# A routed attention block: the extra unit narrowed to 32 tokens, with tokens stationary in four column strips

## The chip, the core and the metric

The kernel runs on one core of a Trainium2 chip. Its time is the device time of one execution in microseconds (us); a measured time is the median of several runs. The core has TensorE (PE in the profile, with PEld for its weight loads), VectorE (DVE), ScalarE (ACT), GpSimd (POOL) and SyncE (SP, whose queue issues most DMAs).

## What is computed

Three layers, of 8 batches with 576 tokens, 8 heads of 64, so 4608 rows of 512 values. First an attention through 32 packed tokens, then two layers that route every token to one of 8 experts; the second adds its input and skips tokens with a low score:

```
p_packed = sm_attn(p, k, v)
out = sm_attn(q, p_packed, p_packed)
...
x = moe(out)     # e = argmax(x @ w_gate); out = gate * (relu(x @ w1[e]) @ w2[e])
x = moe2(x)      # the same for tokens with x @ w_skip > 0, added to x
```

Hidden size F is 1024. With this case's inputs nearly every token of a batch goes to one expert in the first layer: worked out from the reference, 4607 of the 4608 tokens go to the most frequent expert of their batch, and one, token 326 of batch 1, goes to another.

## The kernel before

All products are fp32 or split into two fp32r parts (names ending in h and l, three matmuls for one product). For each batch `gen_S`, `gen_T` and `gen_R` do the attention and the routing, `gen_pre` forms Q1 = packed values times W1 of the batch's common expert, and `gen_M` the main work: `stage1` (line 649, PE `h`, 48 matmuls for each half of 288 tokens) and `stage2` (line 670, PE `y`, 96 matmuls for each half). The classes `Weave` and `merge` lay side generators between the steps of the main one by a position from 0 to 1. The order that the engines get at the end is what the building program's scheduler makes of it, and it can differ from the order in the code.

Tokens that go to another expert than their batch's common one are handled in extra units. A unit is a group of 64 neighbouring tokens of one batch (`UW` = 64, `NU` = 9 to a batch) with one other expert. `x_flags` (lines 878 to 891) counts for each unit and expert whether a token wants it: five matmuls with `M5` (line 881) and a few DVE operations. `gen_prefix` numbers the flagged units, `x_sel` picks one, `x_load` (lines 916 to 936) issues its loads on SP: packed values (`PK`, stored by line 438 to `pkd`), attention weights of the unit (`A2`), gates (`gB`), then W1 of its expert in four DMAs of 512 KB (line 929) and W2 in four of 512 KB (line 934). Here one unit is flagged. `gen_x` computes it, as a side generator of the first half of the last batch (`first_half`, with `NXS` steps from position 0.25 to 1.0):

- Q1 of the unit's expert: 2 x 8 matmuls on eight tiles of the array (line 366, `q<-eW,xPK`, 512 columns), copied to SBUF by DVE and ACT;
- `h`: 16 matmuls with full 128x128 weights and 64 columns (line 957), relu on DVE and ACT in eight pieces;
- `y`: 16 matmuls, tokens as weights in two strips of 64 columns of the array, 256 columns of W2 each (line 967);
- four transposes (977), `L` (982) for the second layer's routing, `route`, and three accumulating DMAs on POOL (986, 989, 993).

Behind it SP issues the loads of the second layer's first expert into the same buffers (`load0`). The stretch from there on is a chain of such experts, up to the end.

The packed values of each batch go to DRAM in `gen_S`: DVE scales them (`pk`, line 430), PE transposes them (434), ACT copies the result out (`PKT`, 437) and issues the store (438).

Of the kernel before, what the change touches and what calls it, by code (L numbers as in the profile page):

```python
# [24 lines left out]
NU = 9  # L25
UW = 64
# [92 lines left out]
def attn_moe_kernel(ctx, tc, q, k, v, p, wg, w11, w12, w21, w22, out):  # L119
# [31 lines left out]
    M5 = ct("M5", [128, 5, NXB])  # L151
# [4 lines left out]
    valx = ct("valx", [NXB, B, 3])  # L156
    valy = ct("valy", [64, 32])
    GM = [ct(f"GM{i}", [128, 5, 32]) for i in range(2)]
    GMx = ct("GMx", [32, 2, 32])
# [28 lines left out]
    def gen_consts():  # L188
        for t, x in ((sel, 0.0), (valy, 0.0), (GMx, 0.0), (FM, 0.0), (FX, 0.0), (csx, 0.0)):
# [4 lines left out]
        stp, q8, m8, bid, R2 = (  # L194
            ct("c_" + n, shp)
            for n, shp in (("stp", [128, 16]), ("q8", [128, 1]), ("m8", [128, 1]), ("bid", [NXB, B]), ("R2", [128, 4, E]))
# [5 lines left out]
        iota_f(bid, [[1, B]], 0, 0)  # L202
# [10 lines left out]
        nc.vector.tensor_copy(valx[:, :, 1], q8[0:NXB, :].to_broadcast([NXB, B]))  # L213
        yield
        nc.vector.tensor_copy(valx[:, :, 2], m8[0:NXB, :].to_broadcast([NXB, B]))
# [9 lines left out]
        for i, c in enumerate(LC):  # L225
            for s in range(i % 2, 5):
                u = (c // 32 + s) // 2
                nc.gpsimd.tensor_copy(
                    M5[32 * i:32 * i + 32, s, E * u:E * u + E], E8[32 * i:32 * i + 32, :]
                )  # L230
            yield
# [139 lines left out]
    def gen_S(b):  # L371
# [66 lines left out]
        nc.scalar.dma_start(out=pkd[b], in_=PKT)  # L438
# [439 lines left out]
    def x_flags():  # L878
        f0 = mt("f0")
        for s in range(5):  # L880
            nc.tensor.matmul(out=f0[0:NXB, 0:B], lhsT=M5[:, s, :], rhs=csA[:, s, :], start=(s == 0), stop=(s == 4))
        FL = X["FL"]
        nc.vector.tensor_scalar(
            out=FL, in0=kmA[0:NXB, :], scalar1=-1.0, scalar2=float(E), op0=ALU.mult, op1=ALU.add
        )
        nc.vector.tensor_tensor(out=FL, in0=FL, in1=valx[:, :, 2], op=ALU.not_equal)
        nc.vector.scalar_tensor_tensor(
            out=FL, in0=f0[0:NXB, 0:B], scalar=0.0, in1=FL, op0=ALU.is_gt, op1=ALU.mult
        )
        nc.tensor.matmul(out=f0[0:32, 64:64 + B], lhsT=ones[0:NXB, 0:32], rhs=FL, start=True, stop=True)  # L890
        nc.vector.tensor_copy(X["cnt"], f0[0:32, 64:64 + B])

    def x_prep(X, b0, nb):
        X["b0"], X["nb"] = b0, nb
        X["fc"] = X["FL"][:, b0:b0 + nb]
        X["pc"] = yield from gen_prefix(X["fc"], nb, NXB)
        nc.vector.memset(X["ctr"], 0.0)

    def x_sel(X):
# [9 lines left out]
            in1=o[:, 0:nb].unsqueeze(1).to_broadcast([NXB, 3, nb]), op=ALU.mult,  # L909
# [3 lines left out]
        nc.tensor.matmul(out=l0[0:64, 0:3], lhsT=ones[0:NXB, 0:64], rhs=r5, start=True, stop=True)  # L913
# [24 lines left out]
    def gen_x(X):  # L938
        li = X["li"]
        A2g = X["A2"]  # L940
        nc.vector.tensor_tensor(out=A2g, in0=A2g, in1=X["gB"].unsqueeze(1).to_broadcast([128, 2, UW]), op=ALU.mult)
        Q1 = EB["X"].rearrange("p t c -> p (t c)")[:, 0:2 * F].rearrange("p (g f) -> p g f", g=2)
        for n in range(2):
            sl = slice(512 * n, 512 * n + 512)
            ps = [mt("q1") for _ in range(2)]
            heads(ps, X["PK"], lambda hp: EB["W1"][:, hp, sl], start=True, stop=True)
            for g in range(2):
                if g:
                    nc.scalar.copy(out=Q1[:, g, sl], in_=ps[g])
# [42 lines left out]
        gT = yield from route("x", L[0:32, 0:UW], 32, 2, GMx, True)  # L992
# [17 lines left out]
    NXS = 4 + 4 + 2 + 2 + 14 + 4  # L1010
# [236 lines left out]
    for b in range(B):  # L1247
# [19 lines left out]
        if b == B - 2:  # L1267
# [8 lines left out]
            for n, shp in (("PK", [128, 128]), ("A2", [128, 2, UW]), ("gB", [128, UW]), ("h", [128, 8, UW]),  # L1276
# [299 lines left out]
```

## Time and profile before

| what | value |
|---|---|
| median of 3 runs | 621.17 us (620.44 to 621.42) |
| the profiled execution | 618.02 us |
| its span, first to last instruction | 616.4 us |
| PE busy in the span | 588.2 us (95%) |
| DVE, ACT, POOL busy | 339.4, 213.3, 133.1 us |
| DMA, mean over the span | 198 GB/s |
| mean granted PE clock | 0.986 |

The profile is of one execution, and it was 3.15 us under the median. Busy shares are means over stages with different limits; what a change is worth in one stage is read from that stage: which work or wait ends last there.

### The profile page before, as it was taken

How to read it: one execution, taken by the hardware profiler on the slowest of the kernel's cores; microseconds unless marked ns; L12 is line 12 of the kernel's file. 1: busy time of each engine (PE TensorE's matmuls, PEld its weight loads, DVE VectorE, ACT ScalarE, POOL GpSimd, SP SyncE). 2: the span in 40 equal slices, each digit the busy share in tenths (PEclk: the TensorE clock that was granted, in tenths of full speed). 3: DMA queues.
4: the chain of work that ended last, by engine and by line, in shares of the span. 5: the costliest groups of instructions: out<-in, count | busy, mean ns of one | idle time of the engine just before them, and what ended most of it. 6: DMA issues, size and time to landing. Idle time of an engine off the chain costs nothing.

```text
span 616.4 us, 14334 instructions
## 1 busy us (share of the span) xinstructions
PE 588.2 (95%) x5737; PEld 529.2 (86%) x5738; DVE 339.4 (55%) x978; ACT 213.3 (35%) x463; POOL 133.1 (22%) x121
## 2 busy tenths in 40 slices
PE   4698999999999999999999999999999899999996
PEld 2287899899989989989988988799999899999796
DVE  2796738738737746845855854346656166253111
ACT  3352542442362343254244134215424135043110
POOL 3123151060150141132123114020301230140032
PEclk9698999999999999999999999999999999999998
DMA  8918788676477566637435415959137581732065
GB/s 341 346 56 311 282 305 325 224 255 240 175 253 252 211 238 237 252 113 283 177 100 216 178 60 191 342 117 401 33 111 281 76 356 27 236 58 113 1 92 64
DMA packets 35994, 122.18 MB, mean 198 GB/s; under 512 B 5696, under 2 KB 15680, under 8 KB 29888
## 3 DMA queue, kind: packets, MB, share of 16 engines
q1 hardware_dynamic: 30064, 113.56, 50.0%
q0 software_dynamic: 3968, 4.98, 6.4%
q10 hardware_dynamic: 1872, 2.49, 1.2%
q8 instruction: 50, 0.82, 0.5%
q14 instruction: 40, 0.33, 0.2%
HBM read 91.62 MB, written 29.39 MB: 196 GB/s over the span
## 4 chain that ended last, share of the span: by engine, by line
PE 68%; issue 11%; another core or an unknown queue 7%; DVE 5%; DMA 4%; POOL 2%; POOLq 1%; ACT 1%; SPq 0%; DVEq 0%; ACTq 0%
PE y L670 33%; PE h L649 18%; PE y L1225 4%; PE q L366 3%; PE s L366 3%; PE L L706 2%; DMA out_dram<-iXR 2%; POOL iW2l L567 1%; PE pv L422 1%; PE at L411 1%; DMA kT<-in_k_dram 1%; DMA W2c<-in_w_dram 1%; PE L L523 1%; DMA W1c<-in_w_dram 1%
## 5 line engine op out<-in xcount | busy, mean ns | idle before, releaser
L670 PE MATMUL y<-hh,W2h 128*128 128x288 f32 x512 | 156.5, 306 | 1.9 <-ACT W2h L566 1.9
L670 PE MATMUL y<-hh,W2l 128*128 128x288 f32 x512 | 151.5, 296 | 0.7 <-DVE W2l L567 0.7
L670 PE MATMUL y<-hl,W2h 128*128 128x288 f32 x512 | 151.8, 296 | 0.0
L670 PEld LDWEIGHTS y<-hh,W2h 128*128 128x128 f32 x512 | 97.0, 189 | 18.9 <-issue 13.5
L567 POOL TENSOR_TENSOR W2l<-W2c,W2h 128x1024 fp32r<-128x1024 f32 x30 | 72.4, 2413 | 156.5 <-ACT W2h L566 121.8
L670 PEld LDWEIGHTS y<-hh,W2l 128*128 128x128 f32 x512 | 97.0, 190 | 1.0 <-DVE W2l L567 1.0
L670 PEld LDWEIGHTS y<-hl,W2h 128*128 128x128 f32 x512 | 96.8, 189 | 0.1
L655 DVE SCALAR_TENSOR_TENSOR hl<-h,hh 128x288 fp32r<-128x288 f32 x128 | 57.9, 455 | 43.4 <-ACT hh L654 43.0
L654 ACT ACTIVATE hh<-h 128x288 fp32r<-128x288 f32 x128 | 52.6, 412 | 80.4 <-PE h L649 80.2
L649 PE MATMUL h<-A2h,Q1h 128*128 128x288 f32 x256 | 78.3, 306 | 0.0
L649 PE MATMUL h<-A2l,Q1h 128*128 128x288 f32 x256 | 75.5, 295 | 0.0
L649 PE MATMUL h<-A2h,Q1l 128*128 128x288 f32 x256 | 75.3, 294 | 0.0
L649 PE MATMUL h<-eXh,eW1h 128*128 128x288 f32 x192 | 57.8, 301 | 3.9 <-issue 3.3
L1225 PE MATMUL y<-ihh,iW2h 128*128 128x288 f32 x192 | 56.8, 296 | 0.0
L1225 PE MATMUL y<-ihh,iW2l 128*128 128x288 f32 x192 | 56.6, 295 | 0.0
L1225 PE MATMUL y<-ihl,iW2h 128*128 128x288 f32 x192 | 56.5, 294 | 0.0
L649 PE MATMUL h<-eXl,eW1h 128*128 128x288 f32 x192 | 56.5, 294 | 0.0
L649 PE MATMUL h<-eXh,eW1l 128*128 128x288 f32 x192 | 56.5, 294 | 0.0
L687 DVE TENSOR_TENSOR y<-y,gB 128x288 f32<-128x288 f32 x64 | 28.6, 447 | 44.7 <-PE y L670 42.1
L649 PEld LDWEIGHTS h<-A2h,Q1h 128*128 128x128 f32 x256 | 48.0, 187 | 3.8 <-issue 2.3
L566 ACT CAST W2h<-W2c 128x1024 fp32r<-128x1024 f32 x32 | 33.6, 1051 | 49.3 <-DMA W2c<-in_w_dram 19.5
L649 PEld LDWEIGHTS h<-A2h,Q1l 128*128 128x128 f32 x256 | 48.1, 188 | 0.0
(289 smaller groups left out, 948.7 us busy)
## 6 DMA issues: line engine op xcount, KB each, us to landing
W2c<-in_w_dram SPq DMA_DIRECT2D x32, 512.0 KB
eW<-in_w_dram SPq DMA_DIRECT2D x8, 2048.0 KB
W1c<-in_w_dram SPq DMA_DIRECT2D x30, 512.0 KB
kT<-in_k_dram SPq DMA_DIRECT2D x7, 1152.0 KB
qT<-in_q_dram SPq DMA_DIRECT2D x7, 1152.0 KB
v<-in_v_dram SPq DMA_DIRECT2D x7, 1152.0 KB
x2d<-y SPq DMA_DIRECT2D x7, 1152.0 KB
out_dram<-y SPq DMA_DIRECT2D x7, 1152.0 KB
```

The costliest lines, as they stand in the source:

```text
L366: nc.tensor.matmul(out=out[x][32 * hp:32 * hp + 32], lhsT=lhsT[64 * x:64 * x + 64, 32 * hp:32 * hp + 32], rhs=rhs(hp)[64 * x:64 * x + 64], ...
L411: nc.tensor.transpose(ats[x][:, 128 * j:128 * j + 128], a1[:, x, 128 * j:128 * j + 128], ident)
L422: nc.tensor.matmul(out=pv[x][32 * hp:32 * hp + 32], lhsT=aT[:, 4 * x + j, 32 * hp:32 * hp + 32], rhs=vm[:, 2 * hp + x, j, :], start=(j == ...
L566: nc.scalar.copy(out=hi, in_=x)
L567: eng.tensor_tensor(out=lo, in0=x, in1=hi.bitcast(F32), op=ALU.subtract)
L649: nc.tensor.matmul(out=ps[:, 0:nr], lhsT=l[:, t, 128 * f:128 * f + 128], rhs=r[:, t, :], start=(n == 0), stop=(n == 3 * kt - 1),)
L654: nc.scalar.activation(out=hh[:, f, :], in_=ps[:, 0:n_], func=ACTF.Relu)
L655: nc.vector.scalar_tensor_tensor(out=hl[:, f, :], in0=ps[:, 0:n_], scalar=0.0, in1=hh[:, f, :].bitcast(F32), op0=ALU.max, op1=ALU.subtract,)
L670: nc.tensor.matmul(out=ps[:, 0:HALF], lhsT=l[:, f, :], rhs=r[:, f, :], start=(n == 0), stop=(n == 23))
L687: nc.vector.tensor_tensor(out=y1[:, t, cols], in0=ps[:, 0:HALF], in1=d["gB"][:, cols], op=ALU.mult)
L706: nc.tensor.matmul(out=L[32 * i:32 * i + 32, 0:LN], lhsT=wgB[:, t, :], rhs=y1[:, t, LC[i]:LC[i] + LN], start=(t == 0), stop=(t == 3),)
L1225: nc.tensor.matmul(out=ps[:, 0:HALF], lhsT=l[:, f, 128 * t:128 * t + 128], rhs=r[:, f, c], start=(n == 0), stop=(n == 23))
```

## The change

Units become 32 tokens wide (`UW` = 32, `NU` = 18). So that a unit and an expert still fit in 72 partitions, `M5`, the flags and the lists get a second index for the even or odd unit of a pair; `x_flags` has two groups of five matmuls, and the prefix over six batches has twelve columns instead of six.

`gen_x` no longer forms Q1. It writes attention weights times gate into a block-diagonal tile `bd` (cleared once), forms the values of the unit's tokens (`xt`, two matmuls with the packed values as weights), multiplies them with W1, the tokens being the weights in four strips of 32 columns of the array (`h`, 16 matmuls of 256 columns), does the relu in one ACT operation, transposes back (`hT`, two), multiplies with W2 in four strips (`y`, 32 matmuls of 128 columns), copies out and transposes once (`ro`). For `xt` the packed values are needed untransposed, so `pkd` now stores `pk`, and its DMA is issued on ACT ahead of the transpose. `NXS` falls from 30 to 25. Stores of whole batches move the same bytes as before; the loads of the unit's `A2` and `gB` and its additions move half of theirs.

```diff
-NU = 9
-UW = 64
+UW = 32
+NU = S // UW
+NXP = NU // 2 * E
...
+        nc.scalar.dma_start(out=pkd[b], in_=pk.rearrange("p x d -> p (x d)"))
...
-        nc.scalar.dma_start(out=pkd[b], in_=PKT)
...
     def x_flags():
         f0 = mt("f0")
-        for s in range(5):
-            nc.tensor.matmul(out=f0[0:NXB, 0:B], lhsT=M5[:, s, :], rhs=csA[:, s, :], start=(s == 0), stop=(s == 4))
+        for z in range(2):
+            for s in range(5):
+                nc.tensor.matmul(
+                    out=f0[0:NXP, B * z:B * z + B], lhsT=M5[:, s, z, :], rhs=csA[:, s, :], start=(s == 0), stop=(s == 4)
+                )
...
     def gen_x(X):
         li = X["li"]
-        A2g = X["A2"]
-        nc.vector.tensor_tensor(out=A2g, in0=A2g, in1=X["gB"].unsqueeze(1).to_broadcast([128, 2, UW]), op=ALU.mult)
-        Q1 = EB["X"].rearrange("p t c -> p (t c)")[:, 0:2 * F].rearrange("p (g f) -> p g f", g=2)
-        for n in range(2):
-            sl = slice(512 * n, 512 * n + 512)
-            ps = [mt("q1") for _ in range(2)]
-            heads(ps, X["PK"], lambda hp: EB["W1"][:, hp, sl], start=True, stop=True)
-            for g in range(2):
-                if g:
-                    nc.scalar.copy(out=Q1[:, g, sl], in_=ps[g])
-                else:
-                    nc.vector.tensor_copy(Q1[:, g, sl], ps[g])
-                yield
-        hx, yx = X["h"], X["y"]
-        for f in range(8):
-            ps = mt("h")
-            for g in range(2):
-                nc.tensor.matmul(out=ps[:, 0:UW], lhsT=Q1[:, g, 128 * f:128 * f + 128], rhs=A2g[:, g, :],
-                                 start=(g == 0), stop=(g == 1))
-            if f % 2:
-                nc.scalar.activation(out=hx[:, f, :], in_=ps[:, 0:UW], func=ACTF.Relu)
-                yield
-            else:
-                nc.vector.tensor_scalar(out=hx[:, f, :], in0=ps[:, 0:UW], scalar1=0.0, scalar2=None, op0=ALU.max)
+        A2g, bd, xt, hr, hx, ro, yx = (X[n] for n in ("A2", "bd", "xt", "hq", "hx", "rq", "y"))
+        for hp in range(4):
+            r = slice(32 * hp, 32 * hp + 32)
+            nc.vector.tensor_tensor(
+                out=bd[r, :, hp, :], in0=A2g[r], in1=X["gB"][r].unsqueeze(1).to_broadcast([32, 2, UW]), op=ALU.mult
+            )
+        yield
+        ps = mt("xt")
+        for x in range(2):
+            nc.tensor.matmul(
+                out=ps[64 * x:64 * x + 64, 0:4 * UW], lhsT=X["PK"][:, 64 * x:64 * x + 64],
+                rhs=bd[:, x].rearrange("p h c -> p (h c)"), start=True, stop=True,
+            )
+        nc.vector.tensor_copy(xt, ps[:, 0:4 * UW].rearrange("p (h c) -> p h c", h=4))
+        yield
+        ps = mt("h")
+        for hp in range(4):
+            for z in range(4):
+                nc.tensor.matmul(
+                    out=ps[UW * z:UW * z + UW, 0:256], lhsT=xt[:, hp, :], rhs=EB["W1"][:, hp, 256 * z:256 * z + 256],
+                    start=(hp == 0), stop=(hp == 3),
+                )
+        nc.scalar.activation(out=hr, in_=ps[:, 0:256], func=ACTF.Relu)
+        yield
+        ps = mt("hT")
+        for j in range(2):
+            nc.tensor.transpose(ps[:, 128 * j:128 * j + 128], hr[:, 128 * j:128 * j + 128], ident)
+        nc.vector.tensor_copy(hx, ps[:, 0:256])
+        yield
         ps = mt("y")
         for f in range(8):
-            for n in range(2):
+            j, z = f % 2, f // 2
+            for n in range(4):
                 nc.tensor.matmul(
-                    out=ps[64 * n:64 * n + 64, 0:256], lhsT=hx[:, f, :], rhs=EB["W2"][:, f, 256 * n:256 * n + 256],
-                    start=(f == 0), stop=(f == 7),
+                    out=ps[UW * n:UW * n + UW, 0:128], lhsT=hx[:, 128 * j + UW * z:128 * j + UW * z + UW],
+                    rhs=EB["W2"][:, f, 128 * n:128 * n + 128], start=(f == 0), stop=(f == 7),
                 )
-            if f % 4 == 3:
-                yield
-        nc.scalar.copy(out=X["ro"][0:UW, 0:256], in_=ps[0:64, 0:256])
-        nc.vector.tensor_copy(X["ro"][0:UW, 256:512], ps[64:128, 0:256])
+        nc.scalar.copy(out=ro, in_=ps[:, 0:128])
+        yield
         ps = mt("ro")
-        for t in range(4):
-            nc.tensor.transpose(ps[:, UW * t:UW * t + UW], X["ro"][0:UW, 128 * t:128 * t + 128], ident[0:UW, 0:UW])
+        nc.tensor.transpose(ps[:, 0:128], ro, ident)
         nc.vector.tensor_copy(yx, ps[:, 0:4 * UW].rearrange("p (t c) -> p t c", t=4))
         yield
...
-        gT = yield from route("x", L[0:32, 0:UW], 32, 2, GMx, True)
+        gT = yield from route("x", L[0:32, 0:UW], 32, 1, GMx, True)
...
-    NXS = 4 + 4 + 2 + 2 + 14 + 4
+    NXS = 7 + 14 + 4
...
+            X["bd"] = X["ro"][:, 256:512].rearrange("p (x h c) -> p x h c", x=2, c=UW)
+            nc.vector.memset(X["bd"], 0.0)
```

The scheduler puts the new operations on PE as follows. Before, the end of the unit (PE, first half of the last batch; `h` of line 957 stands in three such pieces of 4, 8 and 4 matmuls ahead of this, each with six main matmuls `y` of line 670 behind it; `eW_5225` is the unit's W2):

```order
L670 MATMUL y<-hh,W2h 128x288
L670 MATMUL y<-hl,W2h 128x288
L670 MATMUL y<-hh,W2l 128x288
L967 MATMUL y<-eW_5225,xh 64x256 x16
L670 MATMUL y<-hh,W2h 128x288
L670 MATMUL y<-hl,W2h 128x288
L670 MATMUL y<-hh,W2l 128x288
```

After, its beginning on PE: the last main matmuls of `stage1` (now line 655), the products with the unit's values and with its W1 (`eW_5227`), and the first main matmuls of `stage2` (now line 676):

```order
L655 MATMUL h<-A2h,Q1h 128x288
L655 MATMUL h<-A2l,Q1h 128x288
L655 MATMUL h<-A2h,Q1l 128x288
L964 MATMUL xt<-xro,xPK 64x128 x2
L973 MATMUL h<-eW_5227,xro 32x256 x16
L676 MATMUL y<-hh,W2h 128x288
L676 MATMUL y<-hl,W2h 128x288
L676 MATMUL y<-hh,W2l 128x288
```

`xt` and `h` stand back to back, behind the whole of `stage1`, where the first Q1 product stood six main matmuls earlier. Then, still on PE, with the transposes `hT` and six main matmuls ahead of what is shown, the product with W2 (`eW_5228`):

```order
L676 MATMUL y<-hh,W2h 128x288
L676 MATMUL y<-hl,W2h 128x288
L676 MATMUL y<-hh,W2l 128x288
L988 MATMUL y<-eW_5228,xh 32x128 x32
L676 MATMUL y<-hh,W2h 128x288
L676 MATMUL y<-hl,W2h 128x288
L676 MATMUL y<-hh,W2l 128x288
L995 MATMUL ro<-ident,xro 128x128
```

Twelve main matmuls of `stage2` now stand between `h` and `y`, and none ahead of `h`; before, 24 stood ahead of `y`.

On ACT the store of the packed values moves, here in the third batch, between evictions of `h` in `gen_M` (`hh`). Before:

```order
L412 COPY aT<-at 128x512 x2
L414 COPY aT<-at 128x128
L654 ACTIVATE hh<-h 128x288 x8
L437 COPY PKT<-ps 128x128
L438 DMA pkd<-PKT 128x128
L286 ACTIVATE ex<-d 128x40
```

After:

```order
L418 COPY aT<-at 128x512 x2
L420 COPY aT<-at 128x128
L660 ACTIVATE hh<-h 128x288
L437 DMA pkd<-pk 128x128
L660 ACTIVATE hh<-h 128x288 x7
L444 COPY PKT<-ps 128x128
L292 ACTIVATE ex<-d 128x40
```

The store now stands behind the first eviction, ahead of seven, where it stood behind the PKT copy.

## Rows read from the trace of the kernel before

**Rows 1.** The page: busy time, share, instructions by engine.

```profile
PE 588.2 (95%) x5737; PEld 529.2 (86%) x5738; DVE 339.4 (55%) x978; ACT 213.3 (35%) x463; POOL 133.1 (22%) x121
```

**Rows 2.** Chain that ended last, in order of time: start us, us, what.

```profile
85.50 0.87 PE at L411 x8
...
385.87 1.02 PE q L366 x16
...
387.88 1.97 PE q L366 x16
...
390.85 0.84 PE h L957 x8
...
392.54 1.73 PE h L957 x16
...
396.82 3.60 PE y L967 x32
...
411.88 6.42 PE h L649 x48
...
424.70 1.21 PE L L706 x16
```

**Rows 3.** Timeline of PE's weight loads: start, us, line, shape, count, idle before.

```profile
387.81 0.15 PEld L366 LDWEIGHTS q<-eW,xPK 64*32 64x32 f32 x8 [0.17 <-issue]
388.79 0.15 PEld L366 LDWEIGHTS q<-eW,xPK 64*32 64x32 f32 x8 [0.83 <-DMA eW<-in_w_dram]
```

**Rows 4.** Timeline of SP's queue: the four W2 loads of the unit.

```profile
382.06 8.31 SPq L934 DMA_DIRECT2D eW<-in_w_dram  x4
```

**Rows 5.** Stretches: busy us by engine, PE clock, DMA share, GB/s.

```profile
388.80:395.70 6.90, 6.90 (x62) 6.06 (x58) 1.53 (x6) 1.26 (x4) 0.00 (x0) 1.00 1.02 288
```

**Rows 6.** Line 967, the old y: the waits that PE's queue executes (ns, times).

```profile
L967 PEldq EVENT_SEMAPHORE  x2: 51/51/51, 394.5 to 395.7; - x2
```

**Rows 7.** Timeline of ACT in the batch before last.

```profile
332.44 0.41 ACT L654 ACTIVATE hh<-h 128x288 fp32r<-128x288 f32 x1 [1.66 <-PE h L649]
...
334.34 0.26 ACT L437 COPY PKT<-ps 128x128 f32<-128x128 f32 x1
334.64 0.34 ACTq L438 DMA_DIRECT2D pkd<-PKT  x1
```

**Rows 8.** Timeline of PE: the flags, and the start of the last half.

```profile
355.42 0.76 PE L881 MATMUL f<-csA,M 128*72 128x8 f32 x10
356.03 0.38 PE L649 MATMUL h<-A2h,Q1h 128*128 128x288 f32 x1
...
411.72 0.29 PE L649 MATMUL h<-A2h,Q1h 128*128 128x288 f32 x1
```

**Rows 9.** Timeline of DVE in the first batches.

```profile
31.57 0.18 DVE L503 TENSOR_SCALAR sm<-sm 128x18 f32<-128x18 f32 x1
```

**Rows 10.** PE's waits in the whole span: us in total, times, longest.

```profile
PE s L366 <- ACT PKT L437: 0.4, 1, 0.4
```

**Rows 11.** Stretches, columns as in rows 5: around the fall, and a gap.

```profile
49.70:52.90 3.20, 0.84 (x5) 0.38 (x3) 1.58 (x2) 1.94 (x2) 0.00 (x0) 1.00 1.01 412
52.90:56.40 3.50, 3.20 (x13) 3.20 (x14) 3.50 (x6) 0.83 (x2) 2.93 (x1) 0.51 1.03 434
...
486.40:493.30 6.90, 4.23 (x32) 4.03 (x31) 0.59 (x2) 3.21 (x4) 2.19 (x3) 1.00 0.57 92
```

**Rows 12.** Timeline of PE: ends of the two gaps, pace of main matmuls.

```profile
51.94 0.40 PE L670 MATMUL y<-hh,W2h 128*128 128x288 f32 x1 [1.93 <-ACT W2h L566]
...
53.61 0.44 PE L670 MATMUL y<-hh,W2h 128*128 128x288 f32 x1
53.85 0.44 PE L670 MATMUL y<-hl,W2h 128*128 128x288 f32 x1
...
56.43 0.29 PE L670 MATMUL y<-hh,W2h 128*128 128x288 f32 x1
...
491.12 0.37 PE L649 MATMUL h<-eXh,eW1h 128*128 128x288 f32 x1 [2.67 <-issue]
```

More of the change, by code (lines that the diff above doesn't have):

```diff
@@ L150, in attn_moe_kernel @@
     E8 = ct("E8", [128, E])
-    M5 = ct("M5", [128, 5, NXB])
+    M5 = ct("M5", [128, 5, 2, NXP])
     once = ct("once", [128, 5, 32])
@@ L193, in gen_consts @@
         yield
-        stp, q8, m8, bid, R2 = (
+        stp, q8, m8, bid, par, R2 = (
             ct("c_" + n, shp)
-            for n, shp in (("stp", [128, 16]), ("q8", [128, 1]), ("m8", [128, 1]), ("bid", [NXB, B]), ("R2", [128, 4, E]))
+            for n, shp in (("stp", [128, 16]), ("q8", [128, 1]), ("m8", [128, 1]), ("bid", [NXP, 2 * B]), ("par", [NXP, 2 * B]), ("R2", [128, 4, E]))
         )
@@ L201, in gen_consts @@
         iota_f(stp, [[-8, 16]], -8, 1)
-        iota_f(bid, [[1, B]], 0, 0)
+        iota_f(bid, [[1, B], [0, 2]], 0, 0)
+        iota_f(par, [[0, B], [1, 2]], 0, 0)
         yield
@@ L212, in gen_consts @@
         nc.vector.tensor_copy(valx[:, :, 0], bid)
-        nc.vector.tensor_copy(valx[:, :, 1], q8[0:NXB, :].to_broadcast([NXB, B]))
+        nc.vector.scalar_tensor_tensor(
+            out=valx[:, :, 1], in0=q8[0:NXP, :].to_broadcast([NXP, 2 * B]), scalar=2.0, in1=par,
+            op0=ALU.mult, op1=ALU.add,
+        )
         yield
-        nc.vector.tensor_copy(valx[:, :, 2], m8[0:NXB, :].to_broadcast([NXB, B]))
+        nc.vector.tensor_copy(valx[:, :, 2], m8[0:NXP, :].to_broadcast([NXP, 2 * B]))
         nc.vector.tensor_copy(valy[:, 0:1], q8[0:64, :])
@@ L879, in x_flags @@
         f0 = mt("f0")
-        for s in range(5):
-            nc.tensor.matmul(out=f0[0:NXB, 0:B], lhsT=M5[:, s, :], rhs=csA[:, s, :], start=(s == 0), stop=(s == 4))
+        for z in range(2):
[3 more added lines that the diff above has]
+                )
         FL = X["FL"]
+        Fv = FL.rearrange("p (b z) -> p b z", z=2)
         nc.vector.tensor_scalar(
-            out=FL, in0=kmA[0:NXB, :], scalar1=-1.0, scalar2=float(E), op0=ALU.mult, op1=ALU.add
+            out=Fv, in0=kmA[0:NXP, :].unsqueeze(2).to_broadcast([NXP, B, 2]), scalar1=-1.0, scalar2=float(E),
+            op0=ALU.mult, op1=ALU.add,
         )
@@ L887, in x_flags @@
         nc.vector.scalar_tensor_tensor(
-            out=FL, in0=f0[0:NXB, 0:B], scalar=0.0, in1=FL, op0=ALU.is_gt, op1=ALU.mult
-        )
-        nc.tensor.matmul(out=f0[0:32, 64:64 + B], lhsT=ones[0:NXB, 0:32], rhs=FL, start=True, stop=True)
-        nc.vector.tensor_copy(X["cnt"], f0[0:32, 64:64 + B])
+            out=Fv, in0=f0[0:NXP, 0:2 * B].rearrange("p (z b) -> p b z", z=2), scalar=0.0, in1=Fv,
+            op0=ALU.is_gt, op1=ALU.mult,
+        )
+        nc.tensor.matmul(out=f0[0:32, 64:64 + 2 * B], lhsT=ones[0:NXP, 0:32], rhs=FL, start=True, stop=True)
+        nc.vector.tensor_reduce(
+            out=X["cnt"], in_=f0[0:32, 64:64 + 2 * B].rearrange("p (b z) -> p b z", z=2), op=ALU.add, axis=AX.X
+        )
     def x_prep(X, b0, nb):
+        b0, nb = 2 * b0, 2 * nb
         X["b0"], X["nb"] = b0, nb
         X["fc"] = X["FL"][:, b0:b0 + nb]
-        X["pc"] = yield from gen_prefix(X["fc"], nb, NXB)
+        X["pc"] = yield from gen_prefix(X["fc"], nb, NXP)
         nc.vector.memset(X["ctr"], 0.0)
@@ L912, in x_sel @@
         l0 = mt("l0")
-        nc.tensor.matmul(out=l0[0:64, 0:3], lhsT=ones[0:NXB, 0:64], rhs=r5, start=True, stop=True)
+        nc.tensor.matmul(out=l0[0:64, 0:3], lhsT=ones[0:NXP, 0:64], rhs=r5, start=True, stop=True)
         nc.vector.tensor_copy(X["li"], l0[0:1, 0:3])
@@ L1275, in attn_moe_kernel @@
             EB["X"] = ep.tile([128, 4, S], F32, name="eX")
-            for n, shp in (("PK", [128, 128]), ("A2", [128, 2, UW]), ("gB", [128, UW]), ("h", [128, 8, UW]),
-                           ("y", [128, 4, UW]), ("ro", [128, DM]), ("ctr", [NXB, 1]), ("o", [NXB, B]), ("ov", [NXB, 3, B]),
-                           ("r5", [NXB, 3]), ("FL", [NXB, B]), ("cnt", [32, B]), ("pcu", [NXB, B]), ("ppc", [NXB, B]),
+            for n, shp in (("PK", [128, 128]), ("A2", [128, 2, UW]), ("gB", [128, UW]), ("h", [128, DM]), ("y", [128, 4, UW]), ("ro", [128, DM]), ("ctr", [NXP, 1]),
+                           ("o", [NXP, 2 * B]), ("ov", [NXP, 3, 2 * B]), ("r5", [NXP, 3]), ("FL", [NXP, 2 * B]),
+                           ("cnt", [32, B]), ("pcu", [NXP, 2 * B]), ("ppc", [NXP, 2 * B]),
                            ("cT", [32, 32]), ("fl", [32, UW])):
@@ L1348, in early @@
                 us[b]["L"] = mt("L")
-                store(b, 0, 4)
+                store(b, 0, 8)
                 logits(b, 0, 1)
@@ L1354, in attn_moe_kernel @@
             W.run(0.84)
-            store(b, 4, NU, 0, 2)
+            store(b, 8, NU, 0, 2)
             W.run()
@@ L1358, in attn_moe_kernel @@
             W.run()
-    store(B - 1, 4, NU, 2, 3)
-    store(B - 1, 4, NU, 3, 4)
+    store(B - 1, 8, NU, 2, 3)
+    store(B - 1, 8, NU, 3, 4)
     logits(B - 1, 2, 3)
```

18 lines of the change are left out of this document (12 added, 6 removed).

## Prediction

> **What bounds the kernel now.** I read the page first: TensorE (PE) is busy for 95% of the span [rows 1], so time is won only where PE's own row gets shorter or where PE waits. The chain that ended last says the same of the stretch that the change touches: between 378 and 432 us every piece of it is PE work. The extra unit (one pass of `gen_x`, for the single token of batch 1 whose expert is not the batch's common one) stands there as seven pieces between the main matmuls of the last batch [rows 2]: the two Q1 products, 1.02 and 1.97 us; the four pieces of `h`, which make 3.41 us (0.84, 1.73 and once more 0.84); and `y`, 3.60 us. The six matmuls between the two Q1 products are main work. The main matmuls cost 6.42 us for 48, 0.134 us each. The main work of the first half (48 and 96 matmuls, some 19.3 us) and the 1.2 us of a logits group leave about 12.4 us of the 33 us between 378.7 and 411.7 us to the extra unit.
>
> The second thing to see is that the unit's weights come late. The second Q1 product lasts twice as long as the first because its last eight weight loads wait 0.83 us for the fourth chunk of W1, until 388.79 us [rows 3]. Behind that chunk come four chunks of W2, 512 KB each: their issue alone ends at 390.37 us [rows 4], and the DMA engines are full, at 288 GB/s, until 395.7 us [rows 5]. 2.10 MB at that rate is 7.3 us, so the last chunk lands near 396.1 us; the two waits that PE's queue executes for the old `y` are at 394.5 and 395.7 us [rows 6], and the old `y` began at 396.8 us without a wait. I take 395.7 us for the landing. Today this costs nothing, since enough work lies ahead of `y`.
>
> **Part 1, the unit itself.** I follow PE from 385.8 us, where the unit's first product begins now [rows 2]. The order of the changed kernel puts six main matmuls there (0.8 us, to 386.6), then `xt` and `h` back to back. `xt` is two matmuls of 128 columns, about 0.3 us. Between them PE has nothing to do while DVE copies 128x128 values out; the nearest row for that is the PKT copy on ACT, 0.26 us [rows 7], with hand-overs 0.45 us: `h` starts near 387.35. For `h` and `y` I need the price of four column strips side by side. The logits row is that shape (128x32 weights, four strips): 16 matmuls of 160 columns in 1.21 us [rows 2], so 640 columns of four strips, 1.9 ns a column. The old `y`, with two strips, gives 2048 columns in 3.60 us, 1.76 ns; the Q1 product 512 columns in 1.02 us, 2.0 ns. The new `h` (4 x 256) and the new `y` (8 x 128) are 1024 columns each: 1.8 to 2.05 us, I take 1.9, the logits row being the same shape. The first half of `h` ends near 388.3, the second needs the W1 chunk of 388.79, and `h` ends at 389.7. Six main matmuls (390.6) cover the relu on ACT (128x256; the 128x288 one takes 0.41 us, rows 7). Two transposes `hT` (eight take 0.87 us, rows 2) with their switch bring 390.9; six more matmuls, under which DVE copies `hT`, bring 391.75. There PE meets `y`, whose first four matmuls need all four W2 chunks. **PE stands from 391.75 to 395.75 us, 4.0 us of a new wait.** `y` ends at 397.65. Left are 84 main matmuls (12 of the 96 of this half ran before `y`, where 24 did) for 11.2 us, one transpose, `L` and their hand-overs, 0.7 us: the half ends at 409.55 where it ended at 411.72 us, the start of the next half [rows 8]. Gain 2.2 us; without the wait it would be 6.2.
>
> **Part 2, what is added elsewhere.** The flags take ten matmuls instead of five. Five cost PE 355.42 to 356.03 us, 0.61 us, in a stretch where PE is full [rows 8]: 0.6 us more, and everything behind moves with it, the loads of the unit too, since they are issued behind work that PE paces. The twelve prefix additions where there were six lie on DVE, between main evictions, and the order places the last of them ahead of the last eviction before `p0`: nothing. The first batches get two small DVE operations ahead of the reciprocal that POOL waits for, of the kind of [rows 9]: 0 to 0.2 us, I take 0.15. The store to `pkd` now stands ahead of evictions on ACT, and waits there for DVE's `pk`; it takes 0.34 us of the queue, and ACT is idle 1.66 us at that place [rows 7]. PE's list of waits has twelve entries; none is for an eviction of `h`, and the one for the PKT copy is 0.4 us, once [rows 10]: nothing. The larger M5 fill, the cleared `bd` and the smaller units of the DMAs lie beside other work: nothing. The loads for the first expert of the second layer, behind the unit's additions on SP, are issued earlier than before; PE does not wait for them now, so nothing is won by that.
>
> **Part 3, the clock.** [...] A gap of 2.67 us at 488.5 us, between full matmuls, brought no fall [rows 11, 12]. [...] At the lower level a main matmul starts every 0.24 us instead of 0.13 [rows 12]; 3.4 us of it hold 14 matmuls and not 25.5, a loss of 1.5 us; if a part of the low stretch falls into the wait, 0.9 us; if all of `y` lies in it, 1.7. I take 1.4.
>
> [...]
>
> **The sum** is made on the profiled execution (618.02 us, span 616.4), 3.15 us under the median of 621.17 us (620.44 to 621.42); I carry the differences over to the median. -2.2 (unit) +0.6 (flags) +0.15 (first batches) +1.4 (clock) = -0.05: **621.1 us**, no change.
>
> **Rivals.**
> R1, the clock stays up. For it: the gap of 2.67 us that brought no fall, and the moment of a fall may depend on more than the gap. Against it: the fall behind 1.93 us. Then 621.1 - 1.4 = 619.7 us.
> R2, the clock stays low for a second stretch, because `y` and what follows at half speed is again not dense. Another 1.5 us: 622.6 us, slower by 0.23%. It decides from the point where the low level lasts more than 5 us. Against it: the one fall inside the span was over within 3.5 us although PE was not full there [rows 11].
> R3, W2 lands before PE gets there, the wait is absent and the clock stays up: 621.1 - 1.4 - 4.0 = 615.7 us. Against it: the DMA engines have no idle share to give [rows 5].
> R4, the strips do not run side by side, and the change does not do what it says: `h` and `y` then cost four times as much, 5.7 us more each, of which the wait swallows 4.0: 11.4 - 4.0 - 1.4 = 6.0 us more, 627 us. The logits row speaks against it.
>
> **How the numbers follow.** Forecast 0.52, R1 0.25, R2 0.13, R3 0.06, R4 0.04. 0.2% is 1.24 us, about what a measurement of this kernel can tell from no change: below 619.93 is faster, above 622.41 slower. The forecast's own spread (columns at 1.8 or 2.05 ns: 0.25 us for each product, only `y` counting; clock 0.9 to 1.7; first batches 0 to 0.2; the landing 395.7 to 396.7) is 620.2 to 622.3; of its 0.52 I give 0.04 to faster, 0.44 to same, 0.04 to slower. R1 lies on the line: 0.15 faster, 0.10 same. R2: 0.03 same, 0.10 slower. R3 is faster, R4 slower. Faster 0.25, same 0.57, slower 0.18. The range reaches from R1 with half a microsecond below it, 619.2, to R2, 622.7.
>
> **What would show it.** In the new trace: `h` near 1.9 us with a pause at its middle; a gap of about 4 us on PE ahead of the unit's `y`, put down to the DMA of W2; `y` near 1.9 us at full clock or 3.5 at the lower; a granted clock of about 0.5 for some 3.4 us somewhere between 394 and 402 us; the flags at about 1.2 us; the first half ending 1.4 us earlier than before without the fall, and about where it ended with it. I am wrong if the gap is under 2 us (then W2 is faster than its row), or if the clock stays at 1.00 through it.

## The result and the profile after

| kernel | median, us | span of the profiled execution, us |
|---|---|---|
| before | 621.19 (620.44 to 621.42) | 616.4 |
| changed | 613.94 (612.21 to 614.12) | 612.5 |

The ratio is 0.9869, with a 95% interval of 0.985 to 0.9888: 7.25 us faster, where no change (621.1) was forecast and 619.2 was the lower end of the range.

Up to the end of the first layer the trace holds nearly what was forecast. These are the new unit's instructions on PE's timeline of the changed kernel (start us, us, what, count, idle before); they answer to the pieces in [rows 2]:

```profile
387.34 0.44 PE L964 MATMUL xt<-xro,xPK 128*64 128x128 f32 x4
389.64 1.93 PE L973 MATMUL h<-eW,xro 128*32 128x256 f32 x32 [1.86 <-issue]
392.42 0.38 PE L981 MATMUL hT<-ident,xh 128*128 128x128 f32 x2
393.53 0.41 PE L988 MATMUL y<-eW,xh 128*32 128x128 f32 x4
395.13 0.41 PE L988 MATMUL y<-eW,xh 128*32 128x128 f32 x2 [1.19 <-DMA eW<-in_w_dram]
396.69 2.61 PE L988 MATMUL y<-eW,xh 128*32 128x128 f32 x58 [1.15 <-DMA eW<-in_w_dram]
400.11 0.41 PE L995 MATMUL ro<-ident,xro 128*128 128x128 f32 x1
401.34 0.44 PE L1000 MATMUL L<-xy,wgAB 128*32 128x32 f32 x8
```

PE stands for 4.20 us in three parts, and the clock falls behind them. In the stretches of the changed kernel (columns as in [rows 5]) PE was busy for 1.56 of 3.9 us; then come 3.4 us at the lower level, a granted clock of 0.50, with PE full:

```profile
393.90:397.80 3.90, 1.56 (x44) 1.25 (x46) 0.00 (x0) 0.00 (x0) 0.00 (x0) 1.00 0.95 336
397.80:401.20 3.40, 3.40 (x34) 2.90 (x26) 0.29 (x1) 0.27 (x1) 0.03 (x1) 0.50 0.99 412
401.20:404.60 3.40, 3.40 (x31) 3.22 (x30) 2.37 (x15) 0.21 (x1) 2.61 (x3) 1.00 0.68 122
```

The time was won behind the unit. The chain of the changed kernel (start us, us, what) begins the last half at 412.24 (before: 411.88, [rows 2]) and its last logits at 432.84, where before they began at 432.49: 0.35 us later than before. The row of before:

```profile
432.49 1.24 PE L L706 x16
```

The changed kernel then runs into the second layer on PE alone:

```profile
412.24 6.41 PE h L655 x48
...
432.84 1.23 PE L L712 x16
434.08 0.63 issue
434.71 12.88 PE h L655 x96
...
462.51 22.26 PE y L1243 x168
```

In what follows the second layer is counted from its first matmul to PE's last: 434.33 to 610.49 us before, 176.2 us, and 434.71 to 606.47 us in the changed kernel, 171.8 us. At the end of its first item stood the gap of 2.67 us of [rows 11, 12], which the trace puts down to "issue". It is gone. This is the stretch of the changed kernel with the same bounds as in [rows 11], PE busy for 6.90 us of 6.90 instead of 4.23:

```profile
486.40:493.30 6.90, 6.90 (x54) 6.90 (x53) 3.63 (x6) 5.02 (x7) 2.17 (x3) 1.00 0.59 103
```

That gap lies at a branch. The line of code that decides which item comes next, L1499 before and L1522 in the changed kernel, has a COMPARE_BRANCH on each engine (count, shortest/median/longest ns, first and last start). First before, where PE's sequencer (PEldq) spends 3.58 us in it:

```profile
L1499 PEldq COMPARE_BRANCH  x1: 3583/3583/3583, 487.0 to 487.0; - x1
```

then the changed kernel:

```profile
L1522 PEldq COMPARE_BRANCH  x1: 453/453/453, 486.4 to 486.4; - x1
```

The trace also shows transfers of instructions. The page of the changed kernel has two queues of that kind; all 11,501 matmuls and weight loads of PE, with its waits and branches, against 49 transfers of 16 KB on q8 make some 235 or more to a transfer, so I take q8 for the queue that brings PE's instructions:

```profile
PE 582.9 (95%) x5750; PEld 527.4 (86%) x5751; DVE 332.7 (54%) x984; ACT 211.0 (34%) x458; POOL 133.7 (22%) x122
...
q8 instruction: 49, 0.80, 0.5%
q14 instruction: 40, 0.33, 0.2%
```

Before, none ran on q8 from 482.5 to 488.0 us, and one from 488.0 to 489.4, in the middle of the branch (DMA view of that stretch: packets, MB, share):

```profile
q8 instruction: 1, 0.02, 4.4%
```

In the changed kernel one had come at 482.5 to 484.0, ahead of the branch:

```profile
q8 instruction: 1, 0.02, 3.9%
```

### The profile page after: what moved, and what is told of

Same layout as the page of the kernel before. It is cut to its first block, busy times and chain, and to the rows that moved or that the text cites. A ratio compares the mean times of both kernels' runs of the same rounds, so it can differ in the third digit from the quotient of the medians.

```text
span 612.5 us, 14364 instructions
## 1 busy us (share of the span) xinstructions
PE 582.9 (95%) x5750; PEld 527.4 (86%) x5751; DVE 332.7 (54%) x984; ACT 211.0 (34%) x458; POOL 133.7 (22%) x122
## 4 chain that ended last, share of the span: by engine, by line
PE 66%; issue 10%; another core or an unknown queue 7%; DMA 7%; DVE 3%; SPq 3%; POOL 2%; ACT 1%; POOLq 0%; ACTq 0%
PE y L676 31%; PE h L655 19%; PE y L1243 4%; PE q L372 3%; PE s L372 3%; DMA out_dram<-iXR 2%; PE L L712 2%; PE pv L428 1%; PE at L417 1%; SPq L949 1%; DMA eW<-in_w_dram 1%; DMA kT<-in_k_dram 1%; PE L L529 1%; DMA out_dram<-ero 1%
## 5 line engine op out<-in xcount | busy, mean ns | idle before, releaser
L655 PEld LDWEIGHTS h<-A2l,Q1h 128*128 128x128 f32 x256 | 48.1, 188 | 0.4 <-DVE A2l L573 0.4
```

The costliest lines, as they stand in the source:

```text
L655: nc.tensor.matmul(out=ps[:, 0:nr], lhsT=l[:, t, 128 * f:128 * f + 128], rhs=r[:, t, :], start=(n == 0), stop=(n == 3 * kt - 1),)
```

## The theories

**F, code fetch.** The change moves PE's code. Counted over the program with a matmul as two instructions, the second layer's first item starts at instruction 7557 before and at 7572 in the changed kernel (that count is too low where matmuls are fp32, as the experiments show). By this theory PE's branch behind it, 3.58 us against 0.45, waits in the one place for a transfer of its target's code and not in the other; nothing that the unit computes matters. The expectations count in pieces of 256 instructions. The traces have transfers of 16 KB on q8, and in before some 254 of PE's instructions to one (7357 to 29, worked out below), 64.6 bytes each.

**U, the unit.** Its additions end earlier, so the second layer's first loads start 2.4 us earlier (407.18 instead of 409.60 us on SP), and that takes waits away behind it.

Instructions in branches that are not taken tell them apart: they move the code behind them and add nothing to execute.

## Experiments

**Eight matmuls in a branch not taken, old unit (e1).**

```diff
             x_loop(X, 0, cnt2)
+            pad = mt("pad")
+            for _ in range(8):
+                nc.tensor.matmul(out=pad[0:32, 0:8], lhsT=ones[:, 0:32], rhs=ones[:, 0:8], start=True, stop=True)
```

> The kernel before, with eight 32x8 matmuls added in a branch that is not taken (inside the one for further extra units, ahead of the second layer's code): nothing more is executed, but the code of TensorE behind it lies 17 instructions further on, about where the change puts it (15). Theory F (code fetch): the gain of 7 us comes from where TensorE's code lies against its 16 KB instruction transfers, so this alone brings it: no 2.67 us pause of PE at 488 us, span 613 to 613.5 instead of 616.4, timed median 613.5 to 614.5. Theory U (the unit: its lighter work ends earlier, and the second layer's loads, 2.4 us earlier, take waits away behind it): nothing moves, span 616.4, median 621.2 within 0.6. VectorE's code is not moved, so its 3.3 us pause at 436.4 should stay under either.

615.22 us (ratio 0.9904, 0.9875 to 0.9934), span 613.5. The branch takes what it takes in the changed kernel, with the old unit, so F holds for most of the gain:

```profile
L1502 PEldq COMPARE_BRANCH  x1: 453/453/453, 487.6 to 487.6; - x1
```

and the second layer, from its first matmul to PE's last, takes 172.9 us instead of 176.2. The changed kernel needs 171.8; 1.1 us are missing. DVE's pause stayed, as expected, and PE now waits for it (waits of this kernel on PE from 430 us on: us in total, times, longest):

```profile
PE f L798 <- DVE f L751: 0.8, 1, 0.8
```

**The other way round: 120 such matmuls, new unit (e2).**

> The changed kernel, with 120 such matmuls in the branch not taken: TensorE's code behind it lies 242 instructions further on, which in pieces of 256 (16 KB at 64 bytes) is 14 back, so within one instruction of where it lay before the change. Theory F: the 2.67 us pause at 488 comes back, span 615.5 to 617, median 620 to 622, so about the time before the change. Theory U: the unit and its loads are as in the changed kernel, so span 612.5 and median 613.9 within 0.6.

616.72 us (0.9932, 0.9906 to 0.9957), span 615.1. The long branch is back, but at 1.86 us and not 3.6, and the kernel is 2.8 us slower than the changed one and not 7. The place matters with either unit; how much it costs differs.

**64 matmuls, old unit (e4).**

> The kernel before with 64 matmuls in the branch not taken: code 129 instructions on, half a 16 KB piece. Theory F in its narrow form (only a start of the first item's 794 instructions within 26 before the end of a piece makes them need five pieces, and delays the fetch of the next branch): again without the pause, span 613 to 614, median 613.5 to 614.5. Theory F in its wide form (each place has pauses of its own, somewhere): any time from 612 to 622, with issue pauses at other places. Theory U: 621.2 within 0.6.

621.88 us (1.0001, 0.9979 to 1.0022), span 620.4. The branch is long again:

```profile
L1502 PEldq COMPARE_BRANCH  x1: 4406/4406/4406, 487.7 to 487.7; - x1
```

F's narrow form was said to expect none half a transfer further on; but 64 of these matmuls are a whole transfer, as shown below, so it is not refuted. Behind the branch stood something new. The clock fell, with PE at rest ahead of it (stretches, columns as in [rows 5]):

```profile
489.20:492.60 3.40, 0.04 (x1) 0.00 (x0) 0.46 (x1) 1.33 (x2) 0.85 (x1) 0.79 0.32 69
492.60:498.00 5.40, 5.37 (x22) 5.40 (x23) 4.44 (x3) 1.34 (x2) 3.00 (x2) 0.50 1.04 331
498.00:502.00 4.00, 4.00 (x33) 4.00 (x32) 1.14 (x3) 1.12 (x3) 2.11 (x1) 1.00 1.03 439
```

**Before, profiled once more (b1),** to see whether that fall is what its first profile lacks.

> The kernel before once more, for a second profile: its first profiled execution (618.02) lies 3.2 below the median of its timed runs. If what is missing in the first profile is a fall of the granted clock after the 2.67 us pause at 488 (as it stands in the profile of before with 64 matmuls: half speed for 6.83 us from 491.16, worth 3.4), this one shows the long branch of TensorE (3.6 us), then a stretch at half clock within 490 to 500, and a span of 618.5 to 620.5. If not: the branch as in the first profile, no fall behind it, and the time lost elsewhere.

622.56 us, span 620.8. The fall is there: a branch of 4.29 us, PE at rest for 3.2 us, and from 1.1 us behind that 3.4 us at the lower level with 16 matmuls in them, where the next 3.5 us hold 28:

```profile
490.80:494.00 3.20, 0.01 (x1) 0.02 (x1) 0.46 (x1) 1.30 (x2) 0.85 (x1) 1.00 0.26 56
495.10:498.50 3.40, 3.40 (x16) 3.40 (x15) 3.40 (x2) 1.34 (x2) 2.78 (x2) 0.50 1.10 371
498.50:502.00 3.50, 3.50 (x28) 3.50 (x28) 3.50 (x3) 0.82 (x2) 2.04 (x1) 1.00 1.00 421
```

So the 3.15 us between the first profile and its median need not be a constant to carry over. But the fall is only a part of the difference. The second span is 4.4 us longer: 3.0 us of that lie ahead of the seventh batch's first `h` (332.07 instead of 329.07 us), where the low level of the first batches lasted 6.83 us instead of 3.41, and 2.1 us in the second layer (178.25 instead of 176.16), 0.5 of them the longer rest of PE; between the two 0.6 us are gained. What the median executions had is not shown.

**64 and 56 matmuls, new unit (e6, e8); 72, old unit (e9).** The first was meant to have PE's code where the old unit with 64 has it. By the count of two to a matmul that was 16 off (7702 and 7686). The other two were to put it right.

> The changed kernel with 64 matmuls in the branch not taken: TensorE's code 130 instructions on, about where it lies in the kernel before with 64 (one instruction apart, of 256). Theory F: TensorE's branch at the second layer's first item takes 2 us or more instead of 0.45, the second layer 175 to 180 us instead of 171.8, median 617 to 622: the change loses its whole gain although its unit is untouched. Theory U: 613.9 within 0.8.

614.33 us, branch 0.45 us, second layer 171.8 us: no loss, against what F was said to expect (again, 64 are a whole transfer).

> The changed kernel with 56 matmuls in the branch not taken. Counted over TensorE's instructions in the order of the code (a matmul is two), the second layer's first item then starts at 7686, as in the kernel before with 64; with 64 in the changed kernel it starts at 7702, so the two last compared were 16 apart and not one. If the place alone decides (with a period of 128 instructions, 8 KB: starts 5 and 6 over a multiple of 128 were slow, 19 to 22 fast, in seven kernels), TensorE's branch behind this item takes 1.8 to 4.5 us instead of 0.45 and the median is 616 to 621. If it is the changed kernel's shorter or earlier unit that keeps the branch fast: 0.45 us, 613.9 within 1.

617.70 us (0.9925, 0.9898 to 0.9953), branch 2.32 us (it stands at 7686):

```profile
L1525 PEldq COMPARE_BRANCH  x1: 2323/2323/2323, 488.5 to 488.5; - x1
```

> The kernel before with 72 matmuls in the branch not taken: start at 7702 as in the changed kernel with 64. If the place alone decides: branch 0.45 us, second layer 172.5 to 173.5 us (VectorE's pause of 3.07 stays), median 614.5 to 616.5. If the old unit keeps it slow everywhere but at one lucky place: branch over 1.8 us, 620 to 622.

616.39 us (0.9905, 0.9877 to 0.9933), branch 0.36 us (7702). At nearly equal places the two units agree on whether the branch is long.

**Two more places, old unit, one profile each (m1, m2).**

> The kernel before with 24 matmuls in the branch not taken: start at 7606, 54 over a multiple of 128. A profile only, for TensorE's branch: if slow places are a small part of 128 (a start just before a boundary), 0.45 us; if half of them, it may be either.

> The kernel before with 40 matmuls in the branch not taken: start at 7638, 86 over a multiple of 128. As the one with 24: 0.45 us if slow places are a small part, either if they are half.

Branch 0.36 us in both; 614.92 and 616.91 us. In the second, as in e5 below, the clock fell for 3.4 us behind PE's wait at L798 (452.6 us).

**How far the added matmuls move the code.** They are fp32, and the traces have an fp32 matmul with such operands as two matmuls and two weight loads: the five of L881 stand as ten in [rows 8], and their weight loads as ten too. Counted so, PE's matmuls, weight loads, waits and branches between 30.5 and 366.0 us of the first profile of before are some 254 to a transfer of 16 KB, 7357 to 29. By that 8, 24, 40, 64 and 72 matmuls move the code by some 32, 96, 160, 256 and 288 instructions: 64 are a whole transfer, and 72 lie where 8 do. The transfers on q8 bear it out. After the second layer's first matmul they start at 37.5, 54.0 and 59.6 us in before and at 37.8, 54.9 and 62.0 in e4; at 35.9, 49.3 and 54.8 us in e1 and at 36.0, 49.6 and 54.8 in e9. So e4 did not test half a transfer. Whole transfers of 256 left out, the branch is long at before's own place (e4) and 32 instructions before the changed kernel's (e2 and e8). At 32 (e1, e9), 96 (m1) and 160 (m2) past before's place, and at the changed kernel's own (e6), it takes 0.36 to 0.45 us.

**What the branch waits for.** In all five profiles with a long branch it ends 1.34 or 1.35 us after the end of a transfer on q8: in before the transfer runs from 488.31 to 489.30 us and the branch ends at 490.63, in e2 the transfer runs from 487.19 to 488.17 and the branch ends at 489.51. In the thirteen others the last transfer ahead of the branch was over at least 1.9 us before it began. With the old unit the transfer starts 1.3 to 2.1 us behind the branch's start, in e2 and e8 0.3 to 0.5 us ahead of it: that is the difference between 3.6 to 4.4 us and 1.9 to 2.3.

**What is left: DVE (e5, e10, e11).** So far it paused 3.05 to 3.34 us ahead of L726 in every kernel with the old unit and 0.8 us ahead of that line (L732) with the new one. In before:

```profile
439.73 2.12 DVE L726 SCALAR_TENSOR_TENSOR fT<-xgT,once 128x160 f32<-128x160 f32 x1 [3.34 <-issue]
```

The first try moved the target of its branch, with nine memsets beside the eight matmuls:

> The kernel before with the eight matmuls and nine small memsets of VectorE in the branch not taken, so that the code of both engines lies within two instructions of the changed kernel's place. Theory F (code places, VectorE's too): VectorE's pause of 3.07 us before L726 at 436 shrinks to about 0.8 as in the changed kernel, PE's wait of 0.75 for it (L798) goes, and the second layer, from its first matmul to PE's last, takes 171.8 to 172.2 us as in the changed kernel, instead of 172.9 with TensorE's code moved alone and 176.2 before; median 613.5 to 615. Against it: VectorE's pause stays, layer two takes 172.9.

616.38 us (0.9937, 0.9912 to 0.9961); the pause stayed at 3.07 us, so moving the target alone does not take it away. The second try moved the branch too, by 13 memsets of DVE in the branch without an extra unit, ahead of the last batch:

```diff
                 first_half(False)
+                for _ in range(13):
+                    nc.vector.memset(X["ctr"], 0.0)
```

> The kernel before with the eight matmuls in the branch not taken behind the last batch, and 13 memsets of VectorE in the branch without an extra unit (not taken either), which moves VectorE's code from the last batch on, its branch into the second layer with it, 12 instructions further on, to where the changed kernel has it. The place theory: VectorE's pause before L726 goes from 3.07 to about 0.8 us, PE's wait of 0.75 at L798 goes, the second layer takes 171.8 us up to PE's last matmul as in the changed kernel (172.5 to 174.1 with TensorE's code moved alone), median 613.5 to 614.8: the change's whole gain with the old unit. Otherwise, if the old unit's work makes the pause: 3.07 stays, 172.5 to 174, 615 to 616.5.

614.23 us (0.991, 0.988 to 0.9939). The pause is gone (DVE's timeline),

```profile
437.44 0.33 DVE L726 SCALAR_TENSOR_TENSOR fT<-xgT,once 128x160 f32<-128x160 f32 x1 [0.77 <-DVE xgT L267]
```

and the second layer takes 171.8 us, with the old unit. With the new unit and DVE's code moved back, the pause returned:

> The changed kernel with 117 memsets of VectorE in the branch without an extra unit (not taken): VectorE's code 116 further on, in pieces of 128 where the kernel before has it. TensorE's code stays. The place theory: VectorE's pause goes from 0.78 to about 3 us, PE waits 0.4 to 0.8 us at L804, the second layer takes 172.5 to 174 us, median 614.5 to 616. Otherwise: pause 0.78, 171.8, median 613.9 within 0.7.

```profile
437.44 2.42 DVE L732 SCALAR_TENSOR_TENSOR fT<-xgT,once 128x160 f32<-128x160 f32 x1 [3.12 <-issue]
```

The second layer took 172.8 us and PE's wait at L804 came back; yet the median, 614.16 us, did not rise (0.9909, where e10 had 0.991 in the same rounds). The clock fell here at 389 us, under `h`, and the first layer ended 1.7 us sooner than in the changed kernel's first profile, from the same mark (the seventh batch's first `h`, 329.2 us there). The median alone would not have shown what the trace shows.

This pause, too, goes with a transfer. In the nine profiles that have it one of 8 KB on q14, the other queue of the kind, starts 1.1 to 1.4 us behind DVE's branch, and DVE goes on 1.3 to 1.5 us after its end; in the nine without the pause none starts in between. Whose instructions q14 brings is not shown.

**The unit by itself, on one chip, in the same rounds (c1 with the new one, c2 with the old one).**

> The changed kernel again, beside the old unit at the same code places (c2). If the forecast's sum for the unit and what goes with it holds (0.05 us less), the two medians lie within 0.7 us of each other, both 613.5 to 614.8. If the unit itself brings part of the 7 us: this one 1 to 3 us under c2. In its profile either the clock falls while PE waits for the unit's weights (about 389 to 395 us; up to the end of the first layer 102 us from the first h after 328) or behind, over full work (397.8; 103.6 us).

> The old unit with TensorE's and VectorE's code where the changed kernel has it (eight matmuls and 13 memsets in branches not taken), again, in the same rounds as the changed kernel. By the forecast's sum: 613.5 to 614.8, within 0.7 of the changed kernel, no pause over 0.7 us on PE behind 430 us. If the unit brings part of the gain: 615 to 617.

613.50 us (612.46 to 614.92) with the new unit, 614.52 us (613.36 to 615.23) with the old one at nearly the same code places, against 622.23 of before (ratios 0.9862, 0.9842 to 0.9883, and 0.9877, 0.9855 to 0.9899). The medians differ by 1.0 us for the new unit, and the intervals overlap, so a gain by the unit itself is not shown. The traces agree: from the seventh batch's first `h` to the last logits of the first layer PE takes 102.4 to 103.7 us in the ten profiles with the old unit and 101.8 to 103.6 in the six with the new one where the change puts it.

The medians below come from six sets of rounds, in which the kernel before took 620.16 to 622.23 us:

| kernels | unit | PE's branch, us | DVE's pause, us | second layer, us | medians, us |
|---|---|---|---|---|---|
| before (two profiles) | old | 3.58, 4.29 | 3.34, 3.07 | 176.2, 178.2 | 621.19 |
| e4 | old | 4.41 | 3.05 | 179.5 | 621.88 |
| e2, e8 | new | 1.86, 2.32 | 0.77, 0.78 | 174.4, 175.0 | 616.72, 617.70 |
| e1, e9, e5 | old | 0.45, 0.36, 0.45 | 3.07, 3.27, 3.07 | 172.9, 173.0, 174.1 | 615.22, 616.39, 616.38 |
| e11 | new | 0.45 | 3.12 | 172.8 | 614.16 |
| e10, c2 | old | 0.45, 0.45 | 0.77, 0.8 | 171.8, 171.8 | 614.23, 614.52 |
| changed, c1, e6 | new | 0.45, 0.45, 0.45 | 0.78, 0.8, 0.77 | 171.8, 171.8, 171.8 | 613.94, 613.50, 614.33 |

**The unit later (e3): is its own price what its trace shows?**

```diff
-                    sides += [(gen_x(X), NXS, 0.25, 1.0)]
+                    gx = gen_x(X)
+                    sides += [(part(gx, 1), 1, m / 24 - 0.01, m / 24 - 0.01) for m in (7, 8, 11, 12, 17, 18, 19)]
+                    sides += [(gx, 18, 0.8, 1.0)]
```

> The changed kernel with the unit's steps later in the half batch: the first product after 11 main steps instead of 8, the second after 17 instead of 10, by when its weights should have landed (W2's last piece at about 396.7 us). If the unit's price is what its trace shows, its waits of 1.86, 1.19 and 1.15 us are filled with main matmuls and the granted clock does not fall at 397.8 (3.4 us at half speed, worth about 1.7): the half ends at 406 to 407 instead of 412.2, and all of it is kept, so median 608 to 609. Rival: the second layer's first loads (SP, 407 us) are now what the second half and the first item wait for, and 2 to 5 us are given back: 610 to 614. Both take the code places as in the changed kernel (one instruction less).

610.21 us (0.9822, 0.9791 to 0.9853), with e7 below the fastest kernel of the study. The three waits are gone but for 0.39 us, and the clock holds over the whole stretch:

```profile
388.60:404.00 15.40, 14.76 (x179) 12.63 (x179) 4.10 (x14) 1.06 (x3) 0.68 (x1) 1.00 1.02 324
```

From the seventh batch's first `h` to the last logits of the first layer PE takes 98.2 us instead of 103.6, so the waits and the clock cost 5.4 us against the changed kernel's first profile, and 3.7 against the profiles where the clock fell under `h`. Some 0.9 us is given back behind it, where PE waits for the last results of the first layer; the chain that ended last runs there through the second layer's weight load (12.79 us from 410.52) and the work of ACT and DVE on these weights:

```profile
PE h L655 <- DMA x2d<-y: 0.8, 1, 0.8
PE L L712 <- DVE y L693: 0.5, 1, 0.5
```

The same with `h` after 10 and `y` after 15 main steps (e7):

> The kernel with the later unit, with its second product two main steps earlier (after 15 instead of 17) and the routing behind it earlier too, so that the second layer's first loads start at about 407.5 instead of 409.3 us. If these loads are what gave back 0.9 us at 429 to 431 (PE's waits of 0.53 and 0.78), these waits go to 0.5 or less and the median is 609 to 610; if W2's last piece is now late (it landed at about 396.7 in the changed kernel), a wait of 0.5 to 1 stands before the second product and the median is 610 to 611.

610.31 us (0.9838, 0.9806 to 0.9871): the wait of 0.5 is gone, that of 0.9 is not, and `y` takes 2.45 us for 1.96. Nothing is gained over the first.

## Why the prediction was wrong

- **Rows.** The old `h` stood in three pieces on the chain and not four; the sum of 3.41 us is that of three, so nothing hangs on it.
- **Flags.** 0.6 us was forecast. PE's main work stands still from 355.50 to 356.76 us, 1.26 us where it was 0.61 [rows 8]: right.
- **`h` at 1.9 us, `y` at 1.9.** Measured 1.93, and 1.96 for `y` where the clock was up and it ran in one piece (e3). The price of four column strips, taken from the logits row, was right, and R4 did not occur.
- **Start of `h`.** 0.45 us was allowed for DVE's copy between `xt` and `h`; it took 1.86. The copy itself is 0.28 us, but DVE had two main evictions and two steps of a token list ahead of it when `xt` was done at 387.78, and starts it at 389.26:

```profile
387.98 0.42 DVE L661 SCALAR_TENSOR_TENSOR hl<-h,hh 128x288 fp32r<-128x288 f32 x1
388.32 0.30 DVE L732 SCALAR_TENSOR_TENSOR fT<-gT,once 128x160 f32<-128x160 f32 x1
388.66 0.32 DVE L737 TENSOR_REDUCE csB<-fT 128x1 f32<-128x160 f32 x1
388.89 0.45 DVE L661 SCALAR_TENSOR_TENSOR hl<-h,hh 128x288 fp32r<-128x288 f32 x1
389.26 0.28 DVE L968 COPY xro<-xt 128x128 f32<-128x128 f32 x1
```

  The mis-sized term is the hand-over, by 1.4 us; a queue was priced as one instruction. By the rows it cost nothing: W2's last chunk came at 396.69 us in any case, and PE would have stood for that instead.
- **The wait for W2.** 4.0 us, with the last chunk at 395.75 us, was forecast. W2's last chunk was there at 396.69 us; the loads start 0.77 us later (W1 from 379.00 instead of 378.23), as the part on the flags said of them. The waits for W2 were 2.34 us, and 4.20 with that for `h`. The sum of the waits was right, since the landing sets it and not the hand-over; the gap ahead of `y` alone was little over half of the forecast.
- **The clock.** A fall, worth 1.4 us, was forecast. It rested on [rows 11, 12]: behind a gap of 1.93 us the clock was at 0.51, and the new gap was to be longer; the 1.4 us are an estimate from the pace of main matmuls there. It came, 3.4 us at 0.50. Where it starts varies between kernels and executions: at 396.9 to 398.0 us, at or behind the end of the waits (changed, c1, e6), and at 389 to 392 us, under `h`, in e2, e8 and e11, which ended the first layer 1.7 us sooner. R1 and R2 did not occur.
- **The sum.** -0.05 us was forecast for the stretch. With all code places equal it is some -1.0 us by the medians (c1 against c2, not clear of noise), and by the first two profiles +0.35 up to the last logits. This part of the prediction holds within a microsecond.
- **The step that failed** is the sum's first line, "I carry the differences over to the median": it puts the whole kernel behind the first layer at nothing, without a reason, and Part 2 has no term for the place of the code. The gap of 2.67 us at 488.5 us was in the rows, and the prediction used it only as evidence on the clock, without asking what "issue" meant there. It was a branch that waited for a transfer of instructions: 3.58 us before, 0.45 in the changed kernel and, with the old unit, as soon as eight matmuls that are never executed move PE's code. The second layer then takes 172.9 us where it took 176.2, or 178.2 with the clock's fall behind the branch, and 171.8 when DVE's code is moved too. By the medians, each against the kernel before in its own rounds, PE's code alone gives 6.1, 5.4 and 4.4 us (e1, e9, e5); DVE's is worth 1.1 us of the second layer, which the medians do not resolve (5.9 us for e10, 7.7 for c2, both together); for the unit up to 1 us is left. The 3.15 us by which the first profile lay under its median was carried along as a constant; b1 shows that two executions of that kernel differ by more than that, in part by the fall behind this branch.
- **The loads behind the unit.** "Nothing is won by that" was right: with the old unit and its later loads the second layer takes the same 171.8 us (e10, c2), so U fell.
- **The first batches.** 0.15 us can't be seen: up to the seventh batch two profiles of one kernel lie 0.8 to 3.0 us apart (after and c1, before and b1).
- No rival had it. R3 gave a similar time for another reason, and W2 was not in time.

**Open** is why the transfer that the long branch waits for starts earlier against it in e2 and e8 than with the old unit. Open too is how far the slow place reaches: of the 256 instructions of a transfer few places were tried. Whether DVE's pause hangs on its branch or on what lies between branch and target was not told apart.

## What to carry to other kernels

Where a kernel has branches, look up the COMPARE_BRANCH rows of the busiest engine before costing an edit: one of 1.86 to 4.41 us was a wait for code here, instructions added or removed ahead of it turned it on and off, and an edit's gain may be that alone. What counts is the idle time of the engine behind it: PE's next branch (L1504 before) took 2.5 to 2.8 us in the same five profiles, and PE stood for 0.5 us at most. To tell, add instructions to a branch that is not taken and compare at equal code places; compare whole traces by stage, since the edited stretch can be as forecast while the time changes elsewhere. And the price of a hand-over is the queue that the other engine has at that moment, 1.86 us here for a copy of 0.28: the unit was best served by putting it later, behind more main work, until its operands were there.

## What was not expected of the hardware

- The same executed instructions took 615 to 622 us by where PE's code lies, and the second layer 1.1 us more or less by where DVE's lies. PE's branch took 0.36 to 0.45 us or 1.86 to 4.41, and the long ones ended 1.34 or 1.35 us after a 16 KB transfer of instructions.
- The long branch can have a second price: with PE at rest for 2.67 us (before) the clock did not fall, with 3.2 and 3.4 us (b1, e4) it did, one profile each, worth 1.4 us (16 matmuls in 3.4 us where 28 fit in 3.5) and more in e4, where 5.4 us of work ran at the lower level. The length of one gap does not settle it: behind PE's wait of 0.75 us at L798 the clock fell in e5 and m2, and in e1 and e9 it did not.
